# An RWKV-5 attention with a SwiGLU block: the order of small work in three steps of its middle

## The chip, the cores and the metric

One core of a Trainium2 chip runs the whole program in one launch. The time is device microseconds, the median of the runs; lower is better. The engines of the core work side by side and each takes its own instructions strictly in the order in which the program issued them: TensorE (PE: matrix products, and PEld for their weight loads), VectorE (DVE), ScalarE (ACT), GpSimd (POOL), and SyncE (SP), which issues most DMAs here; ScalarE issues some. Engines wait for each other through semaphores.

## The reference

```python
# r, k, v: (4 batches, 8 heads, 768 tokens, 48); w, u: (8, 48)
for t in range(S):
    cur = einsum('bhd,bhe->bhde', u * kt, vt)
    y[:, :, t] = einsum('bhd,bhde->bhe', rt, state + cur)
    state = w[..., None] * state + einsum('bhd,bhe->bhde', kt, vt)
x = y.transpose(0, 2, 1, 3).reshape(3072, 384)
g, val = x @ w_gate, x @ w_val          # 384 -> 1536
out = (silu(g) * val) @ w_out           # 1536 -> 384
```

Attention is a recurrence over tokens with a 48 x 48 state for each batch and head, in fp32. Its output, 3072 tokens by 384, goes through the gated block.

## The kernel before

**Units and steps.** The tokens are cut into 24 units. Units 0 to 9 are 128 tokens of one batch each. From unit 10 on (`PAIRED = 10`) a unit is a pair, 64 tokens of two batches, one in each half of the partitions. `part(i, p)` says which: units 10 and 11 are two successive blocks of 64 tokens of batches 2 and 3, so unit 11 needs the state as unit 10 leaves it; from unit 12 on the two pairs of batches take turns, so a unit needs the state of the unit two before it.

The loop `for s in range(4, N + 2)` (L1463) runs steps. Step s prepares unit s+1 (scaling of k by `scale_k`, the product r*k*u by `own_product`, both on GpSimd), computes the scores of unit s-1 (`scores`, L555 for pairs), the outputs of unit s-2 (`outputs`, L589 for pairs, L654 before), and folds a unit into the state. For pairs that last part is `paired_update`: matmuls (L603) and four additions of their sums to the state on VectorE (L619, two for each batch), after the second and the fourth of which GpSimd multiplies that batch's state by the decay (L622). The state of a pair lies in spare rows of the tile `v_ld`, from which the outputs read it. In step s the update is that of unit s-2, so step 12 folds in unit 10, and step 13 computes the outputs of unit 11. For units 0 to 9 `update` does the same with L679 and L680, and SyncE copies the last states into `v_ld` (L684).

**Score matrices.** `At` of a pair is put together from four sources: the diagonal term (ScalarE scales an identity by the sums `du`, L385, into the region `own_of(i)`, from where `fill_own` copies it by DMA), the turned r (`fill_turned`, two DMAs, L533), the scores from PSUM (four masked copies on VectorE, L563), and the state's rows. The region for the diagonals is in `hv` for units 10 and 11, and from unit 12 on in `zs`, the tile that held the states of units 0 to 9.

**Turning.** From unit 10 on k and r are turned in two parts: `move_blocks` (eight DMAs inside the tile `hats`, L444) and two transposes on VectorE (`turn_block`, L466).

**The gated block** fills TensorE between these parts. Its work stands in the list `todo` as pieces: gate and value products with plain matmuls (L697), six matmuls of a projection in a form that saves products at the price of sums (`project`, L777, with the sums of `h_sums`, L749 to L754), or rounds of the form in `three_beside` (L966), whose weight sums GpSimd makes (L869, L896) and whose results VectorE adds up out of PSUM (L990).

**The hand-written order.** `gaps(s, n)`, called at five places n of a step, decides how many pieces come there. In steps 4 to 11 the table `EARLY` says so ("R": rounding or sums of weights, "F": one piece); from step 12 on the rest is shared out evenly: eleven pieces for step 12, of which three come ahead of its outputs, and eleven for step 13, likewise. `feed(n, pops, lazies)` issues n pieces, and after each of them takes some entries of two queues of small work: `small` (the diagonals, one instruction each, `pops` of them) and `lazy` (`lazies` of them, one more while over nine stand there). Whatever is left in both queues is issued in the next step, ahead of its outputs. From step 12 on a piece takes one lazy, in `EARLY` two.

`after_visit(s)` (L468) makes the queue `lazy` of a step from the masked copies and the sums that `scores` and `paired_update` have put there. Before the change the order is: copy, copy, own term, first transpose, copy, second transpose, copy, and then the four state sums, if any. "Own term" is the sum `du` of the next unit and its diagonals; "second transpose" issues, besides the transpose, the DMAs of `fill_turned`, GpSimd's scaling of r for the next unit (L365), that unit's `move_blocks`, and the loads of the unit three ahead.

In the trace step 11's scores and outputs stand at 112.2 to 114.8 us, those of step 12 at 131.2 to 133.3, those of step 13 at 152.3 to 159.7, those of step 14 at 182.2 to 184.5.

Of the kernel before, what the change touches and what calls it, by code (L numbers as in the profile page):

```python
# [22 lines left out]
def fast(  # L23
# [25 lines left out]
    B, H, S, D = r.shape  # L49
    D2 = 2 * D  # L50
    VW = 2 * D + 16
    HP = H // 2
    R2 = 64 + D
    NCH = S // P
    N = B * NCH
# [9 lines left out]
    dve, pool, act, pe, sp = nc.vector, nc.gpsimd, nc.scalar, nc.tensor, nc.sync  # L65
# [6 lines left out]
    w64 = cst.tile([P, HP, 2], FP32, name="w64")  # L72
# [3 lines left out]
    ident = cst.tile([P, P], FP32, name="ident")  # L76
    mask = cst.tile([P, 2, P], FP32, name="mask")
# [21 lines left out]
    def take():  # L99
        return free.popleft()  # L100
    zs = cst.tile([P, B, HP * D2], FP32, name="zs")
    Z = [zs[:, b].rearrange("p (a x) -> p a x", a=HP) for b in range(B)]
    own = zs[:].rearrange("p b x -> p (b x)")[:, 0 : 2 * H * 64].rearrange(
        "p (i h t) -> p i h t", i=2, h=H
    )
    own_first = hv[:, NR : NR + 4].rearrange("p r t -> p (r t)").rearrange(
        "p (i h t) -> p i h t", i=2, h=H
    )

    def own_of(i):  # L110

        return (own_first if i < PAIRED + B // 2 else own)[:, i % 2]
    r_ld = [cst.tile([P, H, D], FP32, name=f"r_ld{i}") for i in range(2)]
    k_ld = [cst.tile([P, H, D], FP32, name=f"k_ld{i}") for i in range(2)]

# [20 lines left out]
    PAIRED = 10  # L136
# [15 lines left out]
    def load(i):  # L152
        for src, dst in zip((k, r), raw(i)):
            for rows, b, t in pieces_of(i):
                n = rows.stop - rows.start
                sp.dma_start(out=dst[rows], in_=src[b, :, t : t + n, :].rearrange("h t d -> t h d"))
# [106 lines left out]
    def round_weights():  # L263
        if done["act"] > done["pool"]:
            round_pool()
        round_act()
# [15 lines left out]
    def own_sum(i):  # L282
        dus[i] = three.tile([P, H], FP32, name="du", tag="du")
        dve.tensor_reduce(dus[i][:], rks.pop(i), axis=AX.X, op=ALU.add)
# [12 lines left out]
    for e in range(2):  # L297
# [3 lines left out]
        out=u_row, in_=bass.AP(tensor=u.tensor, offset=u.offset, ap=[[0, 1], [1, H * D]]),  # L301
# [9 lines left out]
    def warm(n, bank=None):  # L311
# [14 lines left out]
        out=mask[:, 0], in_=mask[:, 0], compare_op=ALU.is_gt, fill=0.0,  # L326
# [34 lines left out]
    def scale_k(i, on=pool):  # L361
        on.tensor_mul(khat[i % 4][:, :, 0:D], raw(i)[0], kscale)

    def scale_r(i):
        pool.tensor_mul(rhat_of(i)[:, :, 0:D], raw(i)[1], rscale)  # L365
# [89 lines left out]
    def turn_block(i, n):  # L455

        if n == 0:
            turned[i] = three.tile([P, HP, P], FP32, name="rT", tag="rT")
        dst = (kT[i % 2], turned[i])[n]
        if i < PAIRED:  # L460
            merged = hats[:, 6:8].rearrange("p n h x -> p (n h x)").rearrange(
                "p (q n a x) -> p n q a x", q=4, n=2, a=HP
            )
            dve.transpose(dst[:].rearrange("p a (t q) -> p q a t", q=4), merged[:, n])
        else:
            dve.transpose(dst[:].rearrange("p a t -> p (a t)"), blocks[n])  # L466

    def after_visit(s):  # L468

        def turn_second():  # L470
            turn_block(s, 1)
            fill_turned(s)
            if s + 1 < N:
                scale_r(s + 1)
                move_blocks(s + 1)
                if s + 3 < N:
                    load(s + 3)

        def own_term():
            own_sum(s + 1)  # L480
            diagonal(s + 1)

        masked, sums = list(lazy)[:4], list(lazy)[4:]
        if len(masked) < 4:
            masked = [*masked, *(lambda: None for _ in range(4 - len(masked)))]
        lazy.clear()
        lazy.extend([
            *masked[:2], own_term if s + 1 < N else lambda: None,
            lambda: turn_block(s, 0), masked[2], turn_second, masked[3], *sums,
        ])  # L490

    lazy = deque()

# [26 lines left out]
    ident64, mask64 = mask[:, 1, 64:P], mask[:, 1, 0:64]  # L520
# [7 lines left out]
    def fill_turned(i):  # L528

        rT = turned[i][:].rearrange("p a (e t) -> p (a e) t", e=2)  # L530
        for p in range(2):
            there = slice(64 - 64 * p, P - 64 * p)
            sp.dma_start(out=both(i)[there, p], in_=rT[there])  # L533
# [781 lines left out]
    def feed(n, pops=1, lazies=1):  # L1315
        for _ in range(n):
            ready = [k for k, (need, _) in enumerate(todo) if need <= done["pool"] + len(summed)]
            if ready:
                todo.pop(ready[0])[1]()
            for _ in range(min(len(lazy), lazies + (len(lazy) > 9))):  # L1320
                lazy.popleft()()
            for _ in range(min(pops, len(small))):
                small.popleft()()
# [22 lines left out]
    def gaps(s, n):  # L1346

        if s not in EARLY:
            if n == 0:
                coming = 40 * ((s < 14) + (s < 18)) + 14 * (s < 22)  # L1350
                share[0] = -(-(len(todo) + coming) // max(25 - s, 1))
            feed(
                share[0] // 5 + (n < share[0] % 5) - (n == 1 and BLOCKS <= s < PAIRED),
                1,
            )
            return
        for what in EARLY[s][n]:
            if what == "R":
                if done["pool"] < NW:
                    round_weights()  # L1360
                elif len(summed) < 4:
                    weight_sum()
            else:
                feed(1, 3, 2)

    share = [0]
    BLOCKS = 10
# [42 lines left out]
    for e in range(2):  # L1410
        rows = slice(64 * e, 64 * e + 64)
# [30 lines left out]
    ahead = next_chunk("act")  # L1442
# [20 lines left out]
    for s in range(4, N + 2):  # L1463
        if 4 < s <= PAIRED:
            own_sum(s)
        if s == PAIRED:
            diagonal(s)
        late = BLOCKS < s + 1 < N and s % 2 == 0
        if s + 1 == PAIRED:

            for e in range(2):
                rows, o = slice(64 * e, 64 * e + 64), 64 - 64 * e
                act.copy(mask64[rows], mask[rows, 0, 64 * e : 64 * e + 64])
                act.copy(ident64[rows], ident[rows, 64 * e : 64 * e + 64])
                sp.dma_start(out=w64[rows, :, 1 - e], in_=w64[o : o + 64, :, 1 - e])
        if s + 1 == BLOCKS:
            turn(s)
        if s + 1 < N:
            scale_k(s + 1)
            if s < PAIRED and not late:  # L1480
                scale_r(s + 1)
            own_product(s + 1)
            if s + 1 < BLOCKS:
                load_v(s + 1)
            if s < PAIRED and s + 3 < N and not late:
                load(s + 3)
        if s + 1 < BLOCKS:
            turn(s)
        gaps(s, 0)
        if s > N:  # L1490
            outputs(s - 2)
        if 4 <= s - 1 < N:
            flush()
            while lazy:
                lazy.popleft()()
            if s - 2 >= PAIRED:
                outputs(s - 2)
                if s < N:
                    fill_own(s)
            scores(s - 1)  # L1500
            if LATE <= s < PAIRED + 2:
                outputs(s - 2)
                update(s - 2)
                fill_own(s)
            if PAIRED <= s < N:
                if s == PAIRED + 2:
                    load_v(s - 1)
                if s != PAIRED + 1:
                    load_v(s)
                after_visit(s)  # L1510
            gaps(s, 1)
        if BLOCKS <= s < PAIRED:
            turn_block(s, 0)
            feed(1)
            turn_block(s, 1)
        if late and s < PAIRED:
            scale_r(s + 1)
        if s + 2 == PAIRED:
            sp.dma_start(out=scales[64:P, 1:3], in_=scales[0:64, 1:3])
        if BLOCKS <= s + 1 <= PAIRED:  # L1520
            move_blocks(s + 1)
            if s + 1 < PAIRED:
                load_v(s + 1)
        if late and s < PAIRED:
            load(s + 3)
        gaps(s, 2)
        if 4 <= s - 2 < LATE - 2:
            outputs(s - 2)
            update(s - 2)
        if s >= 5 and s % 2:  # L1530
            queue((s - 3) // 2)
        if s < PAIRED:
            diagonal(s)
        if s - 2 >= 4:
            gaps(s, 3)
        gaps(s, 4)
        if s == 11:
            dve.tensor_tensor(bad, held[:], wcol[:], ALU.not_equal)
            dve.tensor_reduce(badc, bad, axis=AX.X, op=ALU.add)
            dve.memset(ones, 1.0)  # L1540
        if s == 12:

            n_ps = next_psum(HP, P)
            pe.matmul(n_ps[0:1, 0, 0:1], badc, ones, start=True, stop=True)
            act.copy(outside, n_ps[0:1, 0, 0:1])
# [435 lines left out]
```

## Time and profile before

| | |
|---|---|
| median of 3 runs | 587.31 us (586.51, 587.31, 594.19) |
| the profiled execution | 589.34 us, of it 587.5 us from the first to the last instruction |
| TensorE busy | 571.3 us (97%) |
| VectorE, GpSimd, ScalarE busy | 427.5, 393.6, 223.1 us |
| mean granted clock of TensorE | 0.992 |
| HBM | 28.31 MB read, 4.72 MB written |

A row of the timeline reads: start, duration, engine and line, operation, tile written and tiles read, partitions by elements, count, and in brackets the idle time of the engine just before, with what ended it. "SPq" and "ACTq" are DMA issues. A row of the stretches reads: start and end, length, busy time of PE, PEld, DVE, ACT and POOL (with counts of instructions), the share of full clock granted to TensorE, the share of the DMA engines' time, GB/s. Durations are of one profiled execution.

### The profile page before, as it was taken

The numbers are of one execution on the slowest core, as the hardware profiler recorded it, in microseconds if no ns is written. First come the engines' busy times: TensorE is split into PE (matmuls) and PEld (weight loads), VectorE is DVE, ScalarE is ACT, GpSimd is POOL, SyncE is SP. The second block draws the span as 40 slices with busy tenths as digits, with TensorE's granted clock in tenths as the row PEclk, the third lists the DMA queues.
The fourth block names the chain that finished last, engine by engine and source line by source line (L and its number), as shares of the span: only waits on it lengthen the run. The fifth ranks groups of instructions, "written<-read, shape, count | busy, mean of one in ns | idle before, by whom it ended". The sixth has DMA issues, their size and how long they took to land.

```text
span 587.5 us, 13712 instructions
## 1 busy us (share of the span) xinstructions
PE 571.3 (97%) x5418; PEld 515.2 (88%) x5418; DVE 427.5 (73%) x753; ACT 223.1 (38%) x532; POOL 393.6 (67%) x395
## 2 busy tenths in 40 slices
PE   8899999999799999999999999999999999999996
PEld 7788888889688889988899988889988899988896
DVE  7787778289197869687879677869357877477672
ACT  3668778222144422343522243521144320233310
POOL 6789877998969845979555979536988960010600
PEclk9999999999799999999999999999999999999998
DMA  7989786455525334545334444220200000200002
GB/s 198 232 230 257 220 251 131 88 96 109 117 45 91 60 60 86 114 81 103 53 72 85 105 91 85 43 47 20 55 1 0 1 1 2 54 2 0 2 1 58
DMA packets 152663, 49.16 MB, mean 84 GB/s; under 512 B 139729, under 2 KB 142802, under 8 KB 152594
## 3 DMA queue, kind: packets, MB, share of 16 engines
q1 hardware_dynamic: 147794, 41.22, 33.2%
q10 hardware_dynamic: 4800, 7.02, 4.4%
q8 instruction: 44, 0.72, 0.5%
q14 instruction: 25, 0.20, 0.1%
HBM read 28.31 MB, written 4.72 MB: 56 GB/s over the span
## 4 chain that ended last, share of the span: by engine, by line
PE 82%; POOL 6%; ACT 4%; DVE 3%; SPq 2%; issue 1%; DMA 1%; POOLq 0%; DVEq 0%; ACTq 0%
PE bank L966 31%; PE bank L777 16%; PE ring L966 13%; PE bank L1199 8%; PE bank L697 4%; PE ring L589 3%; PE ring L555 2%; POOL wgv L261 2%; POOL s L896 1%; PE ring L1199 1%; PE ring L603 1%; ACT bank L213 1%; DMA w_bits<-in_moe_w_out_dram 1%; SPq L444 1%; ACT w_low L219 1%
## 5 line engine op out<-in xcount | busy, mean ns | idle before, releaser
L990 DVE TENSOR_TENSOR hv<-hv,bank 128x512 f32<-128x512 f32 x132 | 87.9, 683 | 47.6 <-PE bank L966 41.8
L697 PE MATMUL bank<-xT,wgv 128*128 128x256 f32 x288 | 66.6, 385 | 1.9 <-POOL wgv L237 1.5
L966 PE MATMUL bank<-xf,wgv 128*128 128x256 f32 x256 | 65.7, 381 | 0.0
L990 ACT COPY hv<-bank 128x512 f32<-128x512 f32 x72 | 40.9, 585 | 62.0 <-PE bank L966 62.0
L697 PEld LDWEIGHTS bank<-xT,wgv 128*128 128x128 f32 x288 | 53.3, 190 | 10.5 <-POOL wgv L237 1.7
L966 PEld LDWEIGHTS bank<-xf,wgv 128*128 128x128 f32 x256 | 48.0, 190 | 6.8 <-DVE kT L1244 0.6
L1253 POOL TENSOR_TENSOR hv<-At,hats 128x512 f32<-128x512 f32 x8 | 10.2, 1274 | 63.7 <-ACT At L1252 63.7
L997 ACT ACTIVATE hv<-hv 128x512 f32<-128x512 f32 (+2 forms) x36 | 22.8, 634 | 51.7 <-DVE hv L990 51.7
L385 ACT ACTIVATE zs<-mask,du 128x64 f32<-128x64 f32 x96 | 29.9, 347 | 20.5 <-DVE hv L790 7.0
L966 PE MATMUL bank<-xT,wgv 128*128 128x256 f32 x144 | 35.5, 379 | 0.0
L777 PE MATMUL bank<-wt,hs 128*128 128x192 f32 x192 | 34.1, 329 | 1.4 <-DVE hs L751 1.4
L966 PE MATMUL bank<-xT,s 128*128 128x256 f32 x152 | 35.1, 379 | 0.0
L777 PE MATMUL bank<-wo,hs 128*128 128x192 f32 x192 | 33.9, 327 | 0.0
L754 POOL TENSOR_TENSOR hs<-hv,hs 128x768 f32<-128x768 f32 x6 | 11.2, 1875 | 32.8 <-DVE hs L751 32.8
L777 PEld LDWEIGHTS bank<-wt,hs 128*128 128x128 f32 x192 | 31.3, 190 | 1.9 <-POOL hats L365 1.6
L777 PE MATMUL bank<-wo,hv 128*128 128x192 f32 x192 | 32.5, 326 | 0.0
L966 PEld LDWEIGHTS bank<-xT,s 128*128 128x128 f32 x152 | 28.9, 190 | 3.9
L896 POOL TENSOR_TENSOR s<-wgv 128x256 f32<-128x256 f32 x39 | 29.9, 784 | 3.4 <-PE bank L777 3.4
L896 POOL TENSOR_TENSOR s<-s,wgv 128x256 f32<-128x256 f32 x39 | 30.2, 775 | 2.9
L777 PEld LDWEIGHTS bank<-wo,hs 128*128 128x128 f32 x192 | 31.7, 190 | 0.5 <-DVE hv L785 0.3
L896 POOL TENSOR_TENSOR s<-s 128x256 f32<-128x256 f32 x39 | 31.5, 807 | 0.9
L777 PEld LDWEIGHTS bank<-wo,hv 128*128 128x128 f32 x192 | 31.6, 190 | 0.4
(238 smaller groups left out, 1438.0 us busy)
## 6 DMA issues: line engine op xcount, KB each, us to landing
hats<-hats SPq DMA_DIRECT2D x112, 64.0 KB, 2.4
w_bits<-in_moe_w_gate_dram SPq DMA_DIRECT2D x6, 768.0 KB, 6.6
w_bits<-in_moe_w_val_dram SPq DMA_DIRECT2D x6, 768.0 KB, 5.9
w_bits<-in_moe_w_out_dram SPq DMA_DIRECT2D x6, 768.0 KB, 6.4
At<-rT SPq DMA_DIRECT2D x28, 128.0 KB, 2.4
At<-zs ACTq DMA_DIRECT2D x24, 128.0 KB, 3.6
k_ld<-in_k_dram SPq DMA_DIRECT2D x28, 96.0 KB, 3.2
r_ld<-in_r_dram SPq DMA_DIRECT2D x28, 96.0 KB, 3.1
```

The lines of the kernel that those rows point to most:

```text
L261: pool.tensor_tensor(dst, dst, low, ALU.add)
L385: lambda h=h: act.activation(own_of(i)[:, slot(i, h), :], ident64, AF.Identity, scale=du[:, h : h + 1])
L555: pe.matmul(ps[p][o : o + 64, n, :], kt[rows, n + HP * g, :], rT[rows, n + HP * g, :], start=True, stop=True, skip_group_check=True,)
L589: pe.matmul(ps[32 * q : 32 * q + 32, cc, 64 * p : 64 * p + 64], *x, start=start, stop=stop, skip_group_check=True,)
L697: pe.matmul(gv[:, o, :].rearrange("p (i t) -> p i t", i=2), wt[:, c, P * f : P * (f + 1)], xT[:, 2 * g % NX : 2 * g % NX + 2, c, :], start ...
L754: on.tensor_sub(s[1], h12, x["s"][1])
L777: pe.matmul(ps, lhs[:, f, :], rhs[:, f, :], start=(f == 0 and n in (0, 1, 4)), stop=(f == FH - 1), skip_group_check=True,)
L896: op(made[o], made[a], made[b])
L966: pe.matmul(ps[:, o], u[:, o], v, start=first and o == 0, stop=True, skip_group_check=True,)
L990: do(out, *(pair_of(wide[a][:]) if isinstance(a, str) else a for a in args))
L997: todo.append((at, lambda: act.activation(gate, gate, AF.Silu)))
L1199: pe.matmul(ps, (h[what][q] if h[what] is D_ else h[what][:, q])[:, f, :], wide["o"][what][:, f, :], start=first and f == 0 and (split or ...
```

## The change

Five edits:

- In step 12 the four state sums of unit 10 stand first in `lazy`, ahead of the copies, instead of last.
- In step 10, in which `lazy` holds the own term and the two transposes only, all of it is issued at once in `after_visit`, instead of piece by piece.
- In the table's steps a piece takes up to three lazies instead of two. Of these steps only step 11 has lazies left for its pieces.
- The diagonals of units 12, 14, ... go to elements 768 to 1279 of `zs` (the states of batch 2 and part of 3), instead of 0 to 511 (batch 0 and part of 1); those of units 13, 15, ... to 0 to 511, instead of 512 to 1023.
- In step 9 four small copies of the mask and the identity on ScalarE, and two DMAs that mirror the decays, are issued after the step's block moves and `gaps(9, 2)`, instead of at its start.

```diff
-    own = zs[:].rearrange("p b x -> p (b x)")[:, 0 : 2 * H * 64].rearrange(
-        "p (i h t) -> p i h t", i=2, h=H
-    )
+    own = [
+        zs[:].rearrange("p b x -> p (b x)")[:, x : x + H * 64].rearrange("p (h t) -> p h t", h=H)
+        for x in (2 * HP * D2, 0)
+    ]
...
-        return (own_first if i < PAIRED + B // 2 else own)[:, i % 2]
+        return own_first[:, i % 2] if i < PAIRED + B // 2 else own[i % 2]
...
+        ahead = sums if s == PAIRED + 2 else []
         lazy.extend([
-            *masked[:2], own_term if s + 1 < N else lambda: None,
-            lambda: turn_block(s, 0), masked[2], turn_second, masked[3], *sums,
+            *ahead, *masked[:2], own_term if s + 1 < N else lambda: None,
+            lambda: turn_block(s, 0), masked[2], turn_second, masked[3],
+            *(sums if not ahead else []),
         ])
+        while s == PAIRED and lazy:
+            lazy.popleft()()
...
-                feed(1, 3, 2)
+                feed(1, 3, 3)
...
-        if s + 1 == PAIRED:
-
-            for e in range(2):
-                rows, o = slice(64 * e, 64 * e + 64), 64 - 64 * e
-                act.copy(mask64[rows], mask[rows, 0, 64 * e : 64 * e + 64])
-                act.copy(ident64[rows], ident[rows, 64 * e : 64 * e + 64])
-                sp.dma_start(out=w64[rows, :, 1 - e], in_=w64[o : o + 64, :, 1 - e])
         if s + 1 == BLOCKS:
             turn(s)
...
         gaps(s, 2)
+        if s + 1 == PAIRED:
+
+            for e in range(2):
+                rows, o = slice(64 * e, 64 * e + 64), 64 - 64 * e
+                act.copy(mask64[rows], mask[rows, 0, 64 * e : 64 * e + 64])
+                act.copy(ident64[rows], ident[rows, 64 * e : 64 * e + 64])
+                sp.dma_start(out=w64[rows, :, 1 - e], in_=w64[o : o + 64, :, 1 - e])
```

## The prediction

> **What bounds the kernel now.** The head of the page comes first, then who TensorE waited for, then the stretches round its longest waits.
>
> ```profile
> span 587.5 us, 13712 instructions
> PE 571.3 (97%) x5418; PEld 515.2 (88%) x5418; DVE 427.5 (73%) x753; ACT 223.1 (38%) x532; POOL 393.6 (67%) x395
> ...
> PE ring L589 <- POOL v_ld L622: 3.7, 2, 3.6
> ```
>
> TensorE is busy for 571.3 of 587.5 us and the change takes no matmul away, so only its 16.2 us of idle time and any stretch at a lower clock can move the end. The longest wait, 3.6 us, is that of the outputs of unit 11 (L589, step 13) for GpSimd's decay of the state (L622). The next one inside the changed steps, 1.4 us, is in step 11 (its row stands below). By stretches, and with the rows of TensorE in step 13 and of one run of 25 rounds later on:
>
> ```profile
> 123.61:127.03 3.42, 2.15 (x13) 2.18 (x14) 3.38 (x5) 2.05 (x9) 3.34 (x4) 1.00 0.17 32
> 150.92:154.33 3.41, 1.51 (x14) 0.89 (x13) 0.71 (x2) 0.59 (x1) 3.17 (x5) 1.00 0.87 185
> 154.33:157.75 3.42, 1.60 (x56) 1.48 (x56) 0.00 (x0) 0.00 (x0) 3.26 (x5) 0.50 0.63 96
> 157.75:161.16 3.41, 3.41 (x74) 3.00 (x69) 0.00 (x0) 0.48 (x1) 3.25 (x5) 0.50 0.45 101
> 152.11:162.23 10.12, 6.40 (x137) 5.58 (x137) 0.59 (x1) 1.07 (x2) 9.57 (x14) 0.66 0.59 112
> 182.25:186.29 4.04, 4.04 (x136) 3.71 (x137) 1.68 (x3) 1.01 (x2) 3.81 (x5) 1.00 0.75 147
> ...
> 152.26 0.32 PE L589 MATMUL ring<-At,v_ld 112*32 112x64 f32 x8 [0.16 <-POOL v_ld L622]
> 156.15 1.72 PE L589 MATMUL ring<-At,v_ld 128*32 128x64 f32 x56 [3.56 <-POOL v_ld L622]
> ...
> 274.57 21.78 PE bank L966 x100
> ```
>
> The columns after the length are busy time of PE, PEld, DVE, ACT and POOL, the granted clock, and DMA. The wait costs more than its 3.6 us: the clock is 0.50 from 154.33 to 161.16, two stretches of 3.41 us, while TensorE runs again from 156.15. The same work (outputs, scores, state products, eight wide matmuls) takes 10.12 us in step 13 and 4.04 in step 14.
>
> **The change part by part.**
>
> *State sums first in step 12.* These rows show how the wait arises:
>
> ```profile
> 147.87 1.11 DVE L619 TENSOR_TENSOR v_ld<-ring,v_ld 48x192 f32<-48x192 f32 x3
> 151.28 0.35 DVE L790 TENSOR_TENSOR hv<-hv,bank 128x192 f32<-128x192 f32 x1 [2.30 <-PE bank L777]
> 151.67 0.36 DVE L619 TENSOR_TENSOR v_ld<-ring,v_ld 48x192 f32<-48x192 f32 x1
> ...
> 141.48 0.72 POOL L896 TENSOR_TENSOR s<-wgv 128x256 f32<-128x256 f32 x1 [2.03 <-PE bank L777]
> 151.38 0.83 POOL L622 TENSOR_TENSOR v_ld<-v_ld,w 48x384 f32<-48x384 f32 x1
> 155.27 0.82 POOL L622 TENSOR_TENSOR v_ld<-v_ld,w 48x384 f32<-48x384 f32 x1
> ...
> 137.50 0.89 DVE L563 COPY_PREDICATED At<-mask,ring 64x256 f32<-64x256 int32 x2
> 145.82 0.70 DVE L466 STREAM_TRANSPOSE rT<-hats 128x512 f32<-128x512 f32 x1
> ```
>
> Step 12 has eleven lazies and eleven feed pieces (eight in step 12, three at the head of step 13), the first taking two. Now the sums come in pieces 7 to 10, so the second decay is issued behind unit 14's scaling. With the change they come in pieces 1 to 3, from 137.50 on. I take the first decay at 139.5, in GpSimd's 2.03 us of idle time before 141.48, and the second three forms later, near 145; both are done 7 us before the outputs want them at 152.11. The wait and its slow stretch go: 10.12 - 4.04 = **-6.1**. VectorE does the same work in another order (four sums of 0.36 forward), and its rows from 137.50 to 149 have no idle time to lose. What is late next: the last masked copy of unit 11 now comes behind piece 16's addition (151.28): 151.28 + 0.35 + 0.44 = 152.07, at the end of the last wide matmul before the outputs, 152.11. I count 0, at most 0.4 if a semaphore falls badly.
>
> *What the same move puts back.* The second transpose of step 12 goes from piece 5 to piece 9, with its DMAs for the turned rows, GpSimd's scaling of r for unit 13, eight block moves and four loads on SyncE.
>
> ```profile
> 148.53 6.64 SPq L444 DMA_DIRECT2D hats<-hats  x8
> 160.35 1.46 SPq L156 DMA_DIRECT2D r_ld<-in_r_dram  x2
> ...
> 168.21 0.70 DVE L466 STREAM_TRANSPOSE kT<-hats 128x512 f32<-128x512 f32 x1
> ```
>
> On GpSimd that scaling now stands behind unit 14's three operations. From about 142.5 (141.48 and the 1.0 that step 11 adds, below), 11 forms of some 0.75, one decay of 0.83 and four operations of 1.0 end near 156, so the moves run from 156 to 161.5 and land near 163.6. VectorE wants them at 168.21 now; with the stall gone at about 163. So it stands still there for some 0.9 us with the additions that free PSUM banks queued behind it. A bank is wanted three rounds after the one that lets it go, 2.6 us (four matmuls a round, 21.78 / 25 = 0.87), so I count **+0.1**, bounds 0 and 2 (SyncE may also be held: its load at 160.35 was, for 3.8 us).
>
> *Three lazies a piece in step 11.*
>
> ```profile
> 113.14 6.14 SPq L444 DMA_DIRECT2D hats<-hats  x8
> 121.29 0.71 DVE L466 STREAM_TRANSPOSE kT<-hats 128x512 f32<-128x512 f32 x1 [1.51 <-DMA hats<-hats]
> 121.92 1.14 DVE L749 TENSOR_TENSOR hs<-hv 128x768 f32<-128x768 f32 x1
> 123.10 1.63 DVE L751 TENSOR_TENSOR hs<-hs,hv 128x768 f32<-128x768 f32 x1
> 124.76 0.45 DVE L563 COPY_PREDICATED At<-mask,ring 64x256 f32<-64x256 int32 x1
> 125.23 0.71 DVE L466 STREAM_TRANSPOSE rT<-hats 128x512 f32<-128x512 f32 x1
> 124.88 2.19 PE L777 MATMUL bank<-wt,hs 128*128 128x192 f32 x12 [1.38 <-DVE hs L751]
> ```
>
> The pieces of step 11 now take (copy, copy, own sum), (transpose, copy, transpose), (copy). The third copy and the second transpose move ahead of the sums L749 and L751, for which TensorE already waits; and the first transpose, in front of them, waits for the block moves. They took 0.45 and 0.71, with a little overlap 1.1 us: TensorE starts its product at 125.98 and idles 2.5 us, **+1.1**. Lower bound 0, if the moves land 1.1 earlier; upper 1.5, with the last copy too. VectorE's total up to 129.8 stays, so nothing later slips.
>
> *And the clock.* Of the stretches of 3.41 us, that of step 11 with 2.15 us of work kept the clock at 1.00; that of step 13 with 1.51 was followed by 0.50. With 2.5 us idle a stretch can be left with 0.9 us of work. If the stretches lie anywhere with equal chance, and the limit is half of one (1.7 us, my choice between 1.51 and 2.15), then (3.41 - 2 x 1.7 + 2.5) / 3.41 = 0.73 of the placements lose the clock. The price is a full stretch at half speed, **+1.7**. The row of 154.33 bears on the limit: the clock was down at 154.33, 1.75 us into the gap that began at 152.58. The Trainium skill ("TensorE: Matmul & The Clock Gate", "HAM oscillation — how this bites in real kernels") states the limit as idle gaps above about 3.4 us; by it the sum would lack this 1.7, and the trace does not agree.
>
> *Step 10's line at once.* The transposes, two row DMAs, the scaling of unit 11's r, eight moves and four loads are issued ahead of two gate pieces and a weight sum. The moves gain nothing:
>
> ```profile
> 103.11 1.00 POOL L276 TENSOR_TENSOR rk<-rk,scales 128x384 f32<-128x384 f32 x1
> 106.65 1.08 POOL L680 TENSOR_TENSOR zs<-zs,w 48x192 f32<-48x192 f32 x2
> 107.17 1.27 SPq L684 DMA_DIRECT2D v_ld<-zs  x2
> 108.49 3.26 SPq L162 DMA_DIRECT2D v_ld<-in_v_dram  x4
> 111.86 1.19 SPq L533 DMA_DIRECT2D At<-rT  x2
> ...
> 104.90 0.42 DVE L704 TENSOR_TENSOR hv<-sgs,bank 128x256 f32<-128x256 f32 x1 [2.40 <-ACT sgs L703]
> ```
>
> SyncE issues without a pause from 107.17, released by L680, which stays in place; the moves at 113.14 are bound by its issue. VectorE now waits there for GpSimd's product (104.11) and then does a sum and two transposes (0.5 and twice 0.7) until about 106.1; behind it the first gate product starts 1.2 later than at 104.90. Two banks take turns, so a product may come one piece late: 0, and at most those +1.2.
>
> *Masks' copies and diagonals.*
>
> ```profile
> 89.13 0.25 ACT L1473 COPY mask<-mask 64x64 f32<-64x64 f32 x1
> 89.95 0.59 ACT L418 COPY kT<-ring 128x512 f32<-128x512 f32 x1
> 90.59 0.43 PE L654 MATMUL ring<-rT,zs 112*32 112x128 f32 x8 [0.36 <-ACT kT L418]
> 124.98 0.83 ACT L385 ACTIVATE zs<-mask,du 128x64 f32<-128x64 f32 x3 [5.03 <-DMA v_ld<-zs]
> ```
>
> Four copies (89.13 to 89.95) leave the front of the copy that holds TensorE for 0.36: **-0.4**. They and their two SyncE DMAs land behind the block moves, where SyncE idles until 107.17 and ScalarE's 0.8 us may delay diagonals that are due 10 us later (0 to +0.4). The diagonals of unit 12 go to states whose DMAs ended 20 us before, so ScalarE's wait of 5.03 goes. TensorE at 124.88 waited for VectorE, not for it: 0.
>
> **Sum:** -6.1 + 0.1 + 1.1 + 1.7 - 0.4 = -3.6. The profiled execution took 589.34 with a span of 587.5; the median of the runs is 587.31, so I take the difference from the median: **583.7**.
>
> **The rivals.**
> - *The clock holds in step 11*, by a kind placement or because its limit is a gap longer than 2.5 us: 583.7 - 1.7 = 582.0. For it: the clock bore 1.4 us here. Against it: the row of 154.33. Chance 0.2. (The page named above would have it so.)
> - *No added wait in step 11*, because moves or sums come 1.1 earlier: -6.1 + 0.1 - 0.4 = 580.9. For it: ScalarE is 0.8 earlier from step 9. Against it: SyncE's unbroken issue. 0.08.
> - *Small waits eat more*: VectorE's stand in step 13, the late copy, step 10's margin, 1.5 to 3 us together: 585 to 587. For it: VectorE has no idle time from 129 to 149; against it: each has a cover of its own. 0.12.
> - *Slower: step 13 is held by the late block moves.* At a stand of VectorE of 0.9 us the banks cover it; beyond 2.6 TensorE idles, and beyond 1.7 us of idle time the clock goes too. If SyncE is held 4 to 5 us more, as it was at 160.35, the stand is 5.5: 2.9 idle and some 2.5 of slow clock, 589.1. It gives the whole gain back from a stand of about 4.5. 0.07.
> - *The change misses*: the second decay still ends after 153. It would need GpSimd 7 us later than I have it; the stall stays, 587.3 + 1.1 + 1.7 - 0.4 = 589.7. 0.03.
>
> **How the numbers follow.** The forecast holds 0.5. The range 581.0 to 588.2 takes in the forecast, the holding clock, the small waits and half of the smaller ones, over 0.8. A measurement tells 2% here, about 12 us, from no change: no case reaches 575.6 or 599, so within 2% has 0.97, faster 0.02, slower 0.01.
>
> **What would show it.** Right: no wait of L589 for L622; L619 near 138 to 141 and L622 near 139.5 and 145; a wait of L777 for L751 of about 2.5 us near 124, with a clock of 0.50 in the stretch behind it; block moves starting near 156; no wait of ScalarE for the state's DMA. The sum is wrong if the wait of step 11 stays at 1.4, if the clock holds, or if TensorE waits for VectorE's evictions near 163 to 170.

## The result and the profile after

The changed kernel takes 584.33 us (median of 20 runs, 581.71 to 587.80) against 588.78 for the kernel before in the same measurement (20 runs, 586.51 to 594.19; the three runs shown ahead of the prediction were at its lower end). The ratio is 0.9907, 95% interval [0.9884, 0.9931]: faster by 0.9%, so the interval leaves out "no change", but the gain is inside the 2% below which the verdict says "same". The ratios here and below are taken over the runs of each kernel (here the means are 584.27 and 589.73) and are not quotients of the two medians, which can differ from them by up to 0.003. The forecast was 583.7, within 581.0 to 588.2. Two single executions of later kernels, 838.74 us (the state sums alone) and 980.22 us (the sums ahead of the transpose), at a mean granted clock of 0.66 and 0.56, are left out of the medians and ratios.

The profiled execution has a span of 583.2 us, 4.3 less than before. Lines of the changed kernel are five higher in this part than those of before (L589 is L594, L622 is L627). The head of its page:

```profile
span 583.2 us, 13717 instructions
PE 570.0 (98%) x5418; PEld 514.1 (88%) x5418; DVE 427.9 (73%) x753; ACT 222.9 (38%) x532; POOL 393.5 (67%) x395
```

Who TensorE waited for (us in total, times, the longest):

```profile
PE bank L782 <- DVE hs L756: 3.0, 1, 3.0
...
PE ring L608 <- issue: 0.5, 1, 0.5
PE ring L659 <- ACT kT L419: 0.3, 1, 0.3
```

The wait for the decay, 3.6 us before, is not in the list any more. The wait of step 11, 1.4 before, is 3.0 and heads it. TensorE's rows, with those of before first at the two places that show how the two executions stand to each other (step 12's outputs, and the ninth wide matmul of step 13):

```profile
131.21 1.11 PE L589 MATMUL ring<-At,v_ld 112*32 112x64 f32 x64
...
162.23 2.75 PE L966 MATMUL bank<-xT,s 128*128 128x256 f32 x12
```

and of the changed kernel:

```profile
90.09 0.43 PE L659 MATMUL ring<-rT,zs 112*32 112x128 f32 x8 [0.35 <-ACT kT L419]
...
125.86 3.87 PE L782 MATMUL bank<-wt,hs 128*128 128x192 f32 x12 [2.96 <-DVE hs L756]
...
133.55 1.11 PE L594 MATMUL ring<-At,v_ld 112*32 112x64 f32 x64
...
154.38 1.11 PE L594 MATMUL ring<-At,v_ld 112*32 112x64 f32 x64
155.42 0.69 PE L560 MATMUL ring<-rT,kT 48*64 48x64 f32 x32
155.93 0.63 PE L608 MATMUL ring<-v_ld,hats 64*64 64x48 f32 x32
156.50 1.99 PE L971 MATMUL bank<-xf,s 128*128 128x256 f32 x8
158.33 2.75 PE L971 MATMUL bank<-xT,s 128*128 128x256 f32 x12
```

At step 12's outputs the changed kernel is 2.3 us late (133.55 against 131.21); at the ninth wide matmul of step 13 it is 3.9 ahead (158.33 against 162.23). So step 13 is worth 6.2 us, and steps before it cost some. Where they cost it is in the stretches (columns as before: length, PE, PEld, DVE, ACT, POOL, clock, DMA):

```profile
122.65:126.07 3.42, 0.46 (x3) 0.24 (x2) 3.34 (x5) 0.00 (x0) 3.34 (x4) 1.00 0.68 134
126.07:129.48 3.41, 3.41 (x12) 3.41 (x12) 3.38 (x5) 0.00 (x0) 3.33 (x3) 0.50 0.67 109
129.48:132.89 3.41, 3.41 (x23) 3.41 (x22) 3.34 (x6) 0.32 (x1) 3.33 (x4) 1.00 0.57 85
```

The wait of 2.96 us fell into one stretch, which held 0.46 us of work, and the next stretch ran at 0.50: the product behind the wait takes 3.87 us instead of 2.19. VectorE shows why the wait grew:

```profile
118.63 0.54 DVE L285 TENSOR_REDUCE du<-rk 128x8 f32<-128x384 f32 x1
121.57 0.71 DVE L467 STREAM_TRANSPOSE kT<-hats 128x512 f32<-128x512 f32 x1 [2.40 <-DMA hats<-hats]
122.30 0.45 DVE L568 COPY_PREDICATED At<-mask,ring 64x256 f32<-64x256 int32 x1
122.76 0.71 DVE L467 STREAM_TRANSPOSE rT<-hats 128x512 f32<-128x512 f32 x1
123.39 0.92 DVE L754 TENSOR_TENSOR hs<-hv 128x768 f32<-128x768 f32 x1
124.35 1.36 DVE L756 TENSOR_TENSOR hs<-hs,hv 128x768 f32<-128x768 f32 x1
```

The copy and the second transpose now stand between the first transpose, which waits for DMAs, and the sums that TensorE wants. In step 12 and behind, VectorE's state sums, GpSimd's decays and SyncE's block moves:

```profile
138.66 0.73 DVE L624 TENSOR_TENSOR v_ld<-ring,v_ld 48x192 f32<-48x192 f32 x2
...
139.56 0.98 POOL L627 TENSOR_TENSOR v_ld<-v_ld,w 48x384 f32<-48x384 f32 x1 [0.81 <-DVE v_ld L624]
143.89 2.46 POOL L901 TENSOR_TENSOR s<-wgv 128x256 f32<-128x256 f32 x3 [3.35 <-PE bank L782]
146.31 1.05 POOL L627 TENSOR_TENSOR v_ld<-v_ld,w 48x384 f32<-48x384 f32 x1
...
157.39 5.41 SPq L445 DMA_DIRECT2D hats<-hats  x8
...
164.56 0.71 DVE L467 STREAM_TRANSPOSE kT<-hats 128x512 f32<-128x512 f32 x1 [0.17 <-DMA hats<-hats]
```

The first decay lies in GpSimd's idle time, the second is done at 147.4, 7 us ahead of the outputs at 154.38, and the late block moves hold VectorE for 0.17 us only.

### The profile page after: what moved, and what is told of

It reads as the page before. It is cut to its first block, busy times and chain, and to the rows that moved or that the text cites. A ratio compares the mean times of both kernels' runs of the same rounds, so it can differ in the third digit from the quotient of the medians.

```text
span 583.2 us, 13717 instructions
## 1 busy us (share of the span) xinstructions
PE 570.0 (98%) x5418; PEld 514.1 (88%) x5418; DVE 427.9 (73%) x753; ACT 222.9 (38%) x532; POOL 393.5 (67%) x395
## 4 chain that ended last, share of the span: by engine, by line
PE 85%; ACT 3%; POOL 3%; DVE 2%; DMA 2%; SPq 2%; issue 1%; POOLq 0%; DVEq 0%; ACTq 0%
PE bank L971 32%; PE bank L782 18%; PE ring L971 13%; PE bank L1204 8%; PE bank L702 4%; PE ring L594 2%; PE ring L560 2%; POOL wgv L262 1%; PE ring L1204 1%; DMA w_bits<-in_moe_w_out_dram 1%; PE ring L608 1%; SPq L445 1%; ACT At L394 1%; DMA hats<-in_r_dram 1%; ACT bank L214 1%
## 5 line engine op out<-in xcount | busy, mean ns | idle before, releaser
L782 PE MATMUL bank<-wt,hs 128*128 128x192 f32 x192 | 35.8, 340 | 3.0 <-DVE hs L756 3.0
L782 PEld LDWEIGHTS bank<-wt,hs 128*128 128x128 f32 x192 | 32.9, 198 | 3.5 <-POOL wgv L874 3.2
```

What stands on the lines that cost most here:

```text
L782: pe.matmul(ps, lhs[:, f, :], rhs[:, f, :], start=(f == 0 and n in (0, 1, 4)), stop=(f == FH - 1), skip_group_check=True,)
```

## The experiments

The theory: the state sums bring the whole gain; three lazies a piece in step 11 give part of it back, by the wait and by the clock; the other edits bring nothing. The ratios settle what the state sums bring; the price of three lazies shows in the traces, but is too small for the ratios to tell. Each ratio below is to the kernel before on the same chip. The first four kernels were measured together (before: 589.32), the last four likewise (before: 590.13).

**The state sums alone.** The kernel before with this edit only:

```diff
+        ahead = sums if s == PAIRED + 2 else []
         lazy.extend([
-            *masked[:2], own_term if s + 1 < N else lambda: None,
-            lambda: turn_block(s, 0), masked[2], turn_second, masked[3], *sums,
+            *ahead, *masked[:2], own_term if s + 1 < N else lambda: None,
+            lambda: turn_block(s, 0), masked[2], turn_second, masked[3],
+            *(sums if not ahead else []),
         ])
```

> The kernel before with the state sums first in step 12, and nothing else of the change. My theory: this edit alone takes away the wait of the outputs of unit 11 and its slow clock, 6.1 us, and the wait of step 11 stays at 1.4 us with the clock at 1.00 there: ratio to the kernel before 0.989 to 0.991. Rival: the sums need room that the other edits make (step 10 handed out at once, three lazies in step 11), and alone they only move the wait to another place: ratio 0.995 to 1.000, with a wait of TensorE above 1.5 us somewhere between 130 and 160 us.

584.01 us, ratio 0.9917 [0.9887, 0.9947], just past the 0.989 to 0.991 expected and as fast as the whole change (0.9907); span of the profile 580.7. The wait for the decay is gone from TensorE's list of waits and that of step 11 is as it was before:

```profile
PE bank L779 <- DVE hs L753: 1.3, 1, 1.3
```

There is no other wait over 0.1 us between 130 and 160 us, so the rival falls: the sums need no room made for them.

**All but the state sums.** The changed kernel with `ahead = []`:

> The changed kernel with the state sums back at the end of step 12's line. My theory: the wait for the decay comes back (3 to 4 us and two stretches of clock 0.50), and the wait of step 11 stays at 2.9 us: about 6 us slower than the changed kernel, ratio to the kernel before 1.000 to 1.006. Rival: the other edits bring a part of the gain, ratio below 0.998.

589.74 us, ratio 1.0016 [0.9993, 1.0039]. In its list of waits both stand side by side:

```profile
PE ring L594 <- POOL v_ld L627: 3.4, 1, 3.4
PE bank L782 <- DVE hs L756: 2.9, 1, 2.9
```

The other edits together bring nothing. One part of the expectation failed: in this profiled execution the clock stayed at 1.00 through both waits. Its stretches say why (those with the waits, and what follows):

```profile
124.22:127.64 3.42, 1.56 (x10) 1.59 (x11) 3.32 (x5) 0.00 (x0) 3.42 (x3) 1.00 0.62 122
127.64:131.05 3.41, 3.41 (x23) 3.41 (x23) 3.38 (x6) 0.32 (x1) 3.25 (x4) 1.00 0.65 100
151.53:154.94 3.41, 1.71 (x16) 1.16 (x14) 0.71 (x2) 0.59 (x1) 3.17 (x5) 1.00 0.88 191
154.94:158.36 3.42, 1.71 (x108) 1.62 (x112) 0.00 (x0) 0.48 (x1) 3.26 (x5) 1.00 0.64 107
```

The wait of 3.41 us was cut in half by the border of two stretches, 1.71 us of work in each; of the wait of 2.85, cut by a border too, the larger part left 1.56 us of work in its stretch. This execution is the exception among its twelve runs: its mean clock is 0.999, that of the other eleven 0.987 to 0.994.

**Two lazies a piece in step 11.** The changed kernel with `feed(1, 3, 2)`:

> The changed kernel with two lazies a piece in step 11, as before. My theory: the wait of step 11 goes back to about 1.4 us and the clock holds at 1.00 there: 1.5 us by the wait and up to 1.4 by the clock, so 1.5 to 3 us faster than the changed kernel, ratio to the kernel before 0.984 to 0.990. Rival: the wait of step 11 is made by the block moves alone and not by what stands behind them; then it stays near 2.9 us and the time is that of the changed kernel.

582.44 us, ratio 0.9902 [0.9872, 0.9931], just past the slow end of what was expected; the profile shows what the theory asked for, a wait of 1.5 in TensorE's list, and a clock of 1.00:

```profile
PE bank L782 <- DVE hs L756: 1.5, 1, 1.5
```

Across the two measurements it is 1.9 us under the changed kernel's 584.33, but by ratios and their intervals the two can't be told apart.

**The sums ahead of the transpose.** Two, one, two, two lazies behind the four pieces of step 11:

```diff
-        for what in EARLY[s][n]:
+        for j, what in enumerate(EARLY[s][n]):
...
-                feed(1, 3, 3)
+                feed(1, 3, 1 if (s, n, j) == (11, 1, 1) else 2)
```

> The changed kernel with two, one, two and two lazies after the four pieces of step 11, so that the sums L754 and L756 stand ahead of the first transpose, which waits for the block moves. My theory: no wait of TensorE in step 11 is left, 1.4 us less than with two lazies a piece and 3 to 4.5 less than in the changed kernel: ratio to the kernel before 0.982 to 0.988. Rival: TensorE then waits as long for the second transpose or the last copy at the head of step 12 (131 to 133 us), and the time is that of two lazies a piece.

582.38 us, ratio 0.9886 [0.9853, 0.9919]. That is just past the 0.982 to 0.988 expected. TensorE does not wait in step 11 at all, and not at the head of step 12, so the wait that the rival names is not there; but the time is that of two lazies, for another reason. In step 13 VectorE reaches its first transpose before the block moves have landed, and the prediction's rival of step 13 sets in. The moves start as soon as GpSimd's scaling of r is done (155.30), and GpSimd, busy throughout, gains nothing by the new order: they start 4.8 us after the outputs of unit 11 (155.33 against 150.54), with two lazies a piece 3.7 us after them (154.39 against 150.71). From its timeline:

```profile
155.33 5.41 SPq L445 DMA_DIRECT2D hats<-hats  x8
...
162.49 0.71 DVE L467 STREAM_TRANSPOSE kT<-hats 128x512 f32<-128x512 f32 x1 [1.94 <-DMA hats<-hats]
...
163.83 1.13 PE L971 MATMUL bank<-xf,wgv 128*128 128x256 f32 x4 [0.55 <-DVE hv L995]
165.18 1.13 PE L971 MATMUL bank<-xT,wgv 128*128 128x256 f32 x4 [0.22 <-DVE hv L995]
```

A stand of 1.94 us costs TensorE 0.77. In the kernel with the state sums alone and in that with two lazies a piece the stands were 0.86 and 0.83, and TensorE lost nothing:

```profile
162.31 0.71 DVE L466 STREAM_TRANSPOSE kT<-hats 128x512 f32<-128x512 f32 x1 [0.86 <-DMA hats<-hats]
...
161.55 0.71 DVE L467 STREAM_TRANSPOSE kT<-hats 128x512 f32<-128x512 f32 x1 [0.83 <-DMA hats<-hats]
```

(Another 1.32 us of this profile are a wait in step 9 for ScalarE's copy L419.)

**And the transposes of step 12 early**, which takes that stand away. On top of the last kernel:

```diff
+        if ahead:
+            s0, s1, s2, s3, m0, m1, own, t0, m2, t1, m3 = lazy
+            lazy.clear()
+            lazy.extend([s0, s1, s2, s3, t0, t1, m0, m1, own, m2, m3])
```

> The kernel with the sums L754 and L756 ahead of the first transpose in step 11, and in step 12 the two transposes directly behind the state sums, ahead of the masked copies and the own term. With the old place in step 12 VectorE stood still for 1.94 us in step 13 for unit 13's block moves, and TensorE lost 0.77 us to it. My theory: the block moves start some 5 us earlier, VectorE does not wait for them, and TensorE does not wait between 155 and 170 us: 0.5 to 1 us less than with the old place, ratio to the kernel before 0.982 to 0.988. Rival: the masked copies of unit 11 are late instead, and its outputs (about 150 us) wait 0.5 us or more for VectorE: no gain.

580.17 us, ratio 0.9833 [0.9805, 0.9861]. By its timeline the block moves start at 148.77, VectorE does not wait for them at 158.89, and TensorE is busy without a break from 147 to 162 us:

```profile
148.77 6.44 SPq L445 DMA_DIRECT2D hats<-hats  x8
...
158.89 0.70 DVE L467 STREAM_TRANSPOSE kT<-hats 128x512 f32<-128x512 f32 x1
...
165.31 0.92 PE L975 MATMUL bank<-xf,s 128*128 128x256 f32 x3 [1.02 <-ACT hv L999]
```

The rival falls. One wait of 1.02 us for an eviction on ScalarE is new, so "no wait between 155 and 170" did not come true. This is the fastest version of all: its interval ends at 0.9861, just under the beginning of the changed kernel's in the same measurement, 0.9895 [0.9864, 0.9926]. Against the kernel that it is built on, 0.9886 [0.9853, 0.9919] in the other measurement, the intervals overlap, so the gain of this last step is shown in the trace and not by the times.

**Only the sums and the order of step 11.** The kernel before with these two edits; step 10, the diagonals' region and the masks' copies as they were:

> The kernel before with the state sums first in step 12 and two, one, two, two lazies after the pieces of step 11; step 10, the diagonals' region and the masks' copies are as before. My theory: those three edits bring nothing to TensorE, so this takes the same time as the version that has them too, within 1 us: ratio to the kernel before 0.985 to 0.990, with ScalarE's wait of about 5 us for the state's DMA still there. Rival: with the two long waits gone one of the three shows, and this is 1 to 3 us slower, with a wait of TensorE for ScalarE or for the masks near 90 or 120 us.

581.89 us, ratio 0.9862 [0.9831, 0.9893]; the version with those three edits has 0.9886 in the other measurement. ScalarE's timeline has its long wait as before, and TensorE has none in step 11:

```profile
124.04 0.83 ACT L385 ACTIVATE zs<-mask,du 128x64 f32<-128x64 f32 x3 [4.92 <-DMA v_ld<-zs]
```

TensorE's wait in step 9 is 0.39 us here, with the masks' copies at their old place. In step 13 it loses 0.82 us behind a stand of VectorE of 1.99, as in the version with 1.94. The rival falls.

**The changed kernel again**, beside these:

> The changed kernel once more, beside the others on one chip: ratio to the kernel before 0.988 to 0.993, with a wait of about 3 us in step 11. If the clock is lost by where the stretches of 3.41 us lie, most of the runs show a mean clock of 0.994 or 0.995 and some 0.997 or more, the latter about 1.7 us shorter; if a wait of 3 us always or never costs the clock, they agree.

584.19 us, ratio 0.9895 [0.9864, 0.9926]. Its stretches show the wait and the clock once more:

```profile
123.76:127.18 3.42, 1.22 (x8) 1.25 (x9) 3.32 (x4) 0.00 (x0) 3.42 (x3) 1.00 0.62 127
127.18:130.59 3.41, 3.41 (x12) 3.41 (x12) 3.38 (x7) 0.32 (x1) 3.33 (x3) 0.50 0.68 104
```

The mean clock of its runs is 0.993 to 0.995 in three (584.39 to 585.52 us) and 0.997 to 0.999 in three (582.00 to 583.99), 2.1 us shorter in the mean. Of the 20 runs of the result, 12 have 0.995 or less. The end of the program, at half clock too, enters these means; the profiles that keep the clock up to there have 0.997 or more. So by these means the clock is lost in some executions of one program and kept in others, though no profile of the changed kernel itself caught one that kept it. The clock is not all that moves the time: of the eight runs of the result with 0.997 or more, three are among the slowest, at 585.80 to 586.40 us.

**Step 10's loads behind its lazies.** In the changed kernel the call of `load_v(10)` goes behind `after_visit(10)`:

> The changed kernel with step 10's four loads of v behind its lazies instead of ahead of them on SyncE. My theory: in the changed kernel step 10's block moves are bound by SyncE's issue, behind these loads; now they start 2.5 us earlier (near 110.3 us), VectorE's first transpose of step 11 starts near 119 and TensorE's wait there falls from 3.0 to about 0.5 us, with the clock at 1.00: 2.5 to 4 us less than the changed kernel. Rival: the moves wait for the scaling of r or for the turned rows, and start no earlier; then the wait stays near 3 us.

582.15 us, ratio 0.9891 [0.9845, 0.9936], against 584.19 for the changed kernel beside it: 2.0 less, somewhat under the 2.5 to 4 expected, and not apart by the intervals. The mechanism is plain in the timeline of its profile, which has a span of 579.3:

```profile
109.06 5.44 SPq L445 DMA_DIRECT2D hats<-hats  x8
...
118.47 0.70 DVE L467 STREAM_TRANSPOSE kT<-hats 128x512 f32<-128x512 f32 x1
```

and in TensorE's list of waits:

```profile
PE bank L782 <- DVE hs L756: 0.7, 1, 0.7
```

The moves start at 109.06 instead of 112.78, and VectorE does not wait for them. So in the changed kernel the moves of step 10 were bound by SyncE's issue, and handing the lazies out at once could not bring them forward.

## Why the prediction was right, and where its terms were off

The forecast stood on one large gain and two prices. The gain is shown by runs with and without the edit; both prices stand in the traces, and the times of the runs can't tell them from nothing.

- *Sums first, -6.1:* measured -6.2 between the two places quoted above (2.34 late, then 3.90 ahead). The sums and decays came within 1.4 us of where they were put (138.7 to 142.2, 139.6, 146.3); the last copy of unit 11 cost nothing.
- *Three lazies in step 11, +1.1:* the wait grew by 1.6 (1.38 to 2.96). The step that was off is what the term left out: TensorE came to the place 0.6 earlier and the block moves did not, since they took 6.80 us of SyncE's issue instead of 6.14 (why is open), so that VectorE's transpose began 0.3 later. The copy and the second transpose added 1.2, about as forecast, and the sums themselves took 0.5 less. The upper bound of 1.5 was too low. The second profile of the changed kernel has 2.85.
- *The clock, +1.7 with a chance of 0.73:* it fell for exactly one stretch in both profiles of the changed kernel, and cost 1.4 by step 12's outputs (2.34 late, of which 0.98 is the later start of the product): the product took 1.7 longer, as forecast, and the two behind it 0.3 less. The sum took the whole 1.7, though by its own chance of 0.73 only 1.2 was due. The rival in which it holds is what some of the other executions show.
- *Late block moves in step 13, +0.1:* they started at 157.4 instead of 156 and VectorE stood 0.17 instead of 0.9, since it came to them at 164.39 instead of 163. The banks' cover is real but smaller than the 2.6 us I gave it: 0.86 cost nothing and 1.94 cost 0.77.
- *Masks' copies, -0.4:* wrong. TensorE waits 0.35 for the same copy as before (the row of 90.09 above). I took the four copies for the cause of the wait because they stood in front of it. Across the kernels the wait was 0.36, 0 and 0.39 with the copies in front, and between 0 and 1.32 without them. What moves it so was not tested and stays open.
- *Step 10 and the diagonals' region, 0:* as forecast. ScalarE's wait of 5 us went and TensorE gained nothing.

The sum was -3.6, a ratio of 0.994 by the three runs; the medians of 20 have -4.45 and the profiles -4.3, so the gain was somewhat larger than forecast. That the time itself came out within 0.7 us is in part luck: the three runs that it was counted from were 1.5 us faster than the median of 20, and the gain was 0.85 too small. Of the profiles' -4.3, -0.5 stood already at the wait in step 9 (it begins at 89.74 instead of 90.22); nearly all of that is no work of the change, for the first gate product starts at 18.75 instead of 19.20, ahead of every edit. Another -0.1 was added until step 11; +1.6 and +1.4 come in step 11 and behind it, -6.2 in step 13, and -0.4 later: a wait of TensorE for "issue" near 205 us is 0.5 long, the row of L608 above, and was 0.9 before. The prediction has no term for it. In every kernel with the state sums first it is 0.5 or less, and 0.9 and 1.0 in the two without; why is open.

The Trainium skill's page "TensorE: Matmul & The Clock Gate" ("HAM oscillation — how this bites in real kernels") has the clock lost at idle gaps above about 3.4 us. The measurement decides otherwise here: a gap of 2.85 us lost it and one of 3.41, at that limit, kept it. What the same page says of the window ("Part 1: The HAM clock gate"), 3413 ns and running freely, agrees with the clock's 126.07 to 129.48 and with the whole numbers of such stretches given below.

## What to carry to other kernels

When small work is reordered on an engine that serves a bound one, look at what each entry waits for: an entry that waits for a DMA is a gate, and nothing that the bound engine wants soon should stand behind it. A stall's price is its length and the slow clock behind it, so two waits of 1.4 us that fall into different stretches can be cheaper than one of 2.9 (this is worked out from the stretches below; no run tried it). And after a wait is taken away, the next thing to come late is often what the same move delayed: here unit 13's block moves, which cost nothing until a second wait was gone as well.

## What the runs showed of the hardware

TensorE's clock is set, as far as these ten profiles show, by its work in stretches of 3.41 us that stand fixed in time, and not by the length of a gap. The clock falls at 154.33 and at 584.41 in the kernel before, 126 stretches of 3.413 us apart, and at 126.07 and 580.04 in the changed one, 133 apart. From the first record of the clock on (near 10 us), every stretch at full clock that had 1.56 us of work or more kept it, and every one with 1.51 or less was followed by 0.50 (0.46, 1.22 and 1.51 in the rows shown). So the limit lies between these two here. A stretch at 0.50 that has 1.60 us of work, as that from 154.33 in the kernel before, does not give the full clock back; one that is full does. Where the border falls in a gap differs from run to run, so the same program can lose some 1.4 to 1.7 us by a half-speed stretch in one run and keep them in the next.
